# Pool tiles in PSUM for the first 32 steps, w2 sum jobs stretched and moved, batch 2 two steps later

## The chip, the cores and the metric

The kernel runs on one core of one Trainium2 chip. The metric is the device time of one execution in microseconds, as the median of several runs. Trace times count from the start of the profiled execution's span. The engines are PE (matmul), PEld (its weight loads), DVE, ACT, POOL and SP; SP and POOL also issue the DMA transfers.

## The reference

An attention with learned memory slots feeds a mixture of four experts, all in float32. Batch 8, 8 heads, sequence 576, head size 64, 32 slots; N = 4608 rows, D = 512, E = 4, F = 1024.

```python
a = softmax(phi, axis=2)                          # over the sequence, 32 slots
k_m = einsum('bhsm,bhsd->bhmd', a, k)
v_m = einsum('bhsm,bhsd->bhmd', a, v)
attn = softmax(q @ k_m.T / sqrt(64), axis=-1)
x = (attn @ v_m).transpose(0, 2, 1, 3).reshape(4608, 512)
p = domain_probs / (domain_probs.sum(-1, keepdims=True) + 1e-9)
for e in range(4):
    h = maximum(x @ w1[e], 0)
    out += p[:, e:e+1] * (h @ w2[e])
```

## The kernel before, in words

**Numbers.** Each float32 operand of a large product is split into a rounded high part (ACT, a cast) and the rest (DVE or POOL, a subtraction), and a product is three matmuls: high x high, high x low, low x high.

**Steps.** Two batches make a pair; four pairs. The first product takes attention weights times a `vw` tile (the slots' values already multiplied by w1), so `x` itself is never built. Pairs 0 and 1 run in 256 steps: 128 per pair, 32 per expert, and in an expert two batches, two halves of their columns, and eight slices `j` of F. `first(s)` (L647 to L649) makes a slice of the hidden layer for 256 or 320 columns, ACT's relu (L659) its high part `h` and DVE (L661) the low part; the piece of a 320-column step that belongs to another row tile goes to `hm`. `second(s)` (L680 to L682) multiplies `h` by w2 into output banks, and its third matmul reads the low part. `first` is emitted two steps ahead of `second`. After eight steps `accumulate` (L700, L702) adds the banks, times `p`, into `acc` on DVE. Pairs 2 and 3 come after step 256, in units of seven multiplications for eight, made from the sums of w2 blocks that are prepared earlier.

**Order.** Each engine executes its instructions in order. The emission of the first `FREE` steps is ordered by a scheduler; from there on it stands as written. `plan[s]` holds what else is emitted in step `s`, between `accumulate` of the step before, `first(s + 2)` and `second(s)`; `at(s, f)` puts something there.

**Sum jobs.** `sums(s, own, e, fh)` prepares half of an expert's w2 for the later units. SP loads two 512 KB pieces into `raw` (L208), DVE makes four sums and differences in place (L231 to L234), ACT casts four times (L220), POOL subtracts four times (L221) and stores four pieces of 512 KB (L226). An `own` job uses buffers of the attention's tiles `a`, `tl` and `ph`; the other kind takes one of the three `AT` buffers and two of the three `kvs` buffers. `JOBS` gives the step of each job's load; job n serves expert n // 2, half n % 2.

**Around them.** In stages that prepare `vw` for other pairs (one begins at step 70, one at step 230), SP loads w1 (L142), ACT and POOL split it (L156, L157), PE multiplies (L585), ACT and DVE write `vst` (L590, L591; the three `kvs` buffers) and POOL stores it (L573, `vwd`). SP brings `vwd` back into `vw` tiles, eight loads of 128 KB at a time (L624), and w2 tiles that an earlier step stored (L193).

**PSUM.** `banks` is one tile over all eight banks; `bank(tag)` hands out a bank from a list, four for `pm`, four for `p2`, and `give` returns it.

Of the kernel before, what the change touches and what calls it, by code (L numbers as in the profile page):

```python
# [9 lines left out]
F32 = mybir.dt.float32  # L10
# [9 lines left out]
P = 128  # L20
# [13 lines left out]

FREE = 36
VW_LOAD_AT = ((20, 25), (28, 32))
# [16 lines left out]
ATT = {  # L53
    2: (22, 48, (92, 96, 100), (97, 101, 104)),
    3: (38, 65, (104, 107, 110), (112, 113, 114)),
# [16 lines left out]
X_BANK, Y_BANK, AB_BANK = 4, 2, 6  # L72
JOBS = (62, 87, 99, 108, 117, PAIR + 28, PAIR + 85, PAIR + 94)
KEEP_AT, W2_AGAIN = 20, 24
# [6 lines left out]
def body(ctx: ExitStack, tc: tile.TileContext, qm, qt, kv, kvt, phi, prob, w1, w1d, w2, out):  # L81
# [3 lines left out]
    dram = pool("dram", space=DRAM)  # L85
    banks = pool("psum", space=PSUM).tile([P, 8, 512], F32, name="banks")
    idle = {"pm": deque(range(4)), "p2": deque(range(4, 8))}
    lent = {}

    def bank(tag, *shape):  # L90
        n = idle[tag].popleft()
        out = banks[:, n, :]
        m = 1
        for d in shape:
            m *= d
        names = "abcd"[:len(shape)]
        out = out[:, :m].rearrange(
            f"p ({' '.join(names)}) -> p {' '.join(names)}", **dict(zip(names, shape))
        )
        lent[id(out)] = tag, n, out  # L100
        return out

    def give(ps):
        tag, n, _ = lent.pop(id(ps))
        idle[tag].append(n)

# [89 lines left out]
    def sums(s, own, e, fh):  # L196
# [33 lines left out]
        at(s, load)  # L230
        at(s + 3, lambda: v.tensor_add(kept[1][:, :, low], kept[0][:, :, low], kept[1][:, :, low]))  # L231
        at(s + 3, lambda: sub(kept[0][:, :, low], kept[0][:, :, top], kept[0][:, :, low]))
        at(s + 4, lambda: sub(kept[0][:, :, top], kept[1][:, :, low], kept[0][:, :, top]))
        at(s + 4, lambda: sub(kept[1][:, :, top], kept[1][:, :, top], kept[0][:, :, top]))  # L234
        for i in range(2):
            for j in range(2):
                at(s + 4 + 2 * i + j, lambda i=i, j=j: high(i, j))
            at(s + 6 + 2 * i, lambda i=i: store(i))

# [470 lines left out]
    def at(s, unit):  # L710
        plan[s].append(unit if isinstance(unit, tuple) else (None, unit))
# [116 lines left out]
    for n, s in enumerate(JOBS):  # L828
        sums(s, s != PAIR + 28, n // 2, n % 2)
    for s in FIRST_LOADS:  # L830
# [384 lines left out]

    steps(0, FREE)
    with tc.manual_schedule():
        steps(FREE, BEGIN - 3)
# [61 lines left out]
```

## Time and profile before

| | us |
|---|---|
| median of 3 runs | 1411.86 (1411.23 to 1415.82) |
| profiled execution | 1409.54, span 1407.4 |
| mean granted clock | 0.994 |
| PE busy | 1366.8 (97% of the span) |
| DVE, ACT, POOL busy | 837.9, 624.8, 621.4 |

PE is the engine that is nearly always busy. In a row of waits, the three numbers are the total, the count and the longest. In a row of the timeline, the first number is the start, the second the duration, and the bracket tells how long the engine stood idle before and what ended that.

### The profile page before, as it was taken

The page shows a single profiled execution, that of the slowest core. Times are in us where ns is not written, and L with a number is a line of the kernel's source. Part 1 is how long each engine was busy: PE and PEld are TensorE (multiplying, and loading weights), DVE is VectorE, ACT ScalarE, POOL GpSimd, SP SyncE. Part 2 cuts the span into 40 slices and gives each one's busy share as a digit, 9 for nine tenths or more (in the row PEclk, how much of TensorE's full clock was granted, in tenths as well). Part 3 has the DMA queues.
Part 4 walks back from the last instruction along what each step waited for, and adds up shares of the span by engine and source line. Part 5 has one row for each costly group of instructions (what it writes and reads, how often), then busy time and mean ns, then how long its engine had stood idle before and what let it go on. Part 6 is the DMA issues. An engine that isn't in the chain of part 4 may idle for free.

```text
span 1407.4 us, 25235 instructions
## 1 busy us (share of the span) xinstructions
PE 1366.8 (97%) x8894; PEld 1250.2 (89%) x8894; DVE 837.9 (60%) x1894; ACT 624.8 (44%) x1536; POOL 621.4 (44%) x660
## 2 busy tenths in 40 slices
PE   7899999999999999999979999999999999999998
PEld 6688888888878888889868999899999999999998
DVE  7775545446754365354434467777667666666665
ACT  7654555433444364463225354555543333333332
POOL 4410344755552334422245276676763334333333
PEclk9999999999999999999989999999999999999999
DMA  7832327799684264444588898999985776666662
GB/s 252 272 104 84 123 85 246 228 354 318 226 313 163 90 226 145 139 140 124 188 272 292 278 311 289 314 315 331 321 306 154 223 190 179 177 180 177 178 177 80
DMA packets 102029, 301.37 MB, mean 214 GB/s; under 512 B 24976, under 2 KB 26128, under 8 KB 101904
## 3 DMA queue, kind: packets, MB, share of 16 engines
q1 hardware_dynamic: 81168, 224.26, 51.3%
q0 software_dynamic: 20736, 75.51, 13.8%
q8 instruction: 71, 1.16, 0.4%
q14 instruction: 54, 0.44, 0.1%
HBM read 213.46 MB, written 84.93 MB: 212 GB/s over the span
## 4 chain that ended last, share of the span: by engine, by line
PE 58%; DMA 1%; DVE 1%; ACT 0%; issue 0%; POOL 0%; SPq 0%; DVEq 0%; ACTq 0%
PE banks L1008 22%; PE banks L922 5%; PE banks L923 5%; PE banks L924 5%; PE banks L682 3%; PE banks L680 3%; PE banks L681 3%; PE banks L585 2%; PE banks L647 2%; PE banks L648 2%; PE banks L649 2%; PE banks L1046 1%; PE banks L1047 1%; PE banks L1048 1%; PE banks L469 1%; PE banks L363 1%
## 5 line engine op out<-in xcount | busy, mean ns | idle before, releaser
L1026 DVE SCALAR_TENSOR_TENSOR acc<-banks,pt,acc 128x256 f32<-128x256 f32 x416 | 200.0, 481 | 108.9 <-PE banks L1008 105.2
L157 POOL TENSOR_TENSOR w<-stage,w 128x512 fp32r<-128x512 f32 x134 | 176.6, 1323 | 166.0 <-ACT w L156 153.9
L682 PE MATMUL banks<-w,h 128*128 128x512 f32 x512 | 201.9, 395 | 14.3 <-DVE h L661 14.3
L661 DVE SCALAR_TENSOR_TENSOR h<-banks,h 128x256 fp32r<-128x256 f32 x256 | 107.6, 420 | 164.3 <-ACT h L659 101.6
L680 PE MATMUL banks<-w,h 128*128 128x512 f32 x512 | 202.2, 395 | 1.7 <-DVE acc L702 1.3
L681 PE MATMUL banks<-w,h 128*128 128x512 f32 x512 | 201.7, 394 | 0.0
L659 ACT ACTIVATE h<-banks 128x256 fp32r<-128x256 f32 x256 | 97.8, 384 | 193.1 <-PE banks L649 152.2
L647 PE MATMUL banks<-AT,vw 128*128 128x256 f32 (+1 forms) x512 | 157.4, 308 | 5.7 <-ACT kvs L351 2.2
L1008 PE MATMUL banks<-w,a 128*128 128x256 f32 x1080 | 154.6, 282 | 0.3 <-DVE acc L1026 0.2
L648 PE MATMUL banks<-AT,vw 128*128 128x256 f32 (+1 forms) x512 | 151.7, 297 | 0.0
L922 PE MATMUL banks<-AT,vw 128*128 128x256 f32 (+1 forms) x512 | 151.6, 296 | 0.0
L649 PE MATMUL banks<-AT,vw 128*128 128x256 f32 (+1 forms) x512 | 151.2, 296 | 0.1
L923 PE MATMUL banks<-AT,vw 128*128 128x256 f32 (+1 forms) x512 | 151.1, 295 | 0.0
L924 PE MATMUL banks<-AT,vw 128*128 128x256 f32 (+1 forms) x512 | 150.9, 295 | 0.0
L1008 PEld LDWEIGHTS banks<-w,a 128*128 128x128 f32 x1080 | 143.6, 188 | 4.9 <-issue 0.9
L989 POOL TENSOR_TENSOR vt<-ph,vt 128x512 fp32r<-128x512 f32 x64 | 84.1, 1314 | 107.3 <-ACT vt L988 78.3
L682 PEld LDWEIGHTS banks<-w,h 128*128 128x128 f32 x512 | 96.5, 189 | 37.4 <-DVE h L661 16.0
L352 POOL TENSOR_TENSOR kvs<-stage,kvs 128x512 fp32r<-128x512 f32 x58 | 75.8, 1325 | 101.4 <-ACT kvs L351 100.9
L647 PEld LDWEIGHTS banks<-AT,vw 128*128 128x128 f32 x512 | 97.1, 190 | 18.0 <-DVE vw L562 4.0
L680 PEld LDWEIGHTS banks<-w,h 128*128 128x128 f32 x512 | 96.6, 189 | 13.7 <-DVE acc L702 1.8
L681 PEld LDWEIGHTS banks<-w,h 128*128 128x128 f32 x512 | 96.6, 189 | 11.0
L156 ACT CAST w<-stage 128x512 fp32r<-128x512 f32 x168 | 102.7, 619 | 6.3 <-DMA stage<-in_w 4.1
(149 smaller groups left out, 2985.6 us busy)
## 6 DMA issues: line engine op xcount, KB each, us to landing
w<-kw SPq DMA_DIRECT2D x93, 512.0 KB, 5.3
vwd<-vst POOLq DMA_DIRECT2D x80, 512.0 KB, 6.2
vw<-vwd SPq DMA_DIRECT2D x320, 128.0 KB, 5.7
w<-v SPq DMA_DIRECT2D x55, 512.0 KB, 5.5
stage<-in_w SPq DMA_DIRECT2D x44, 512.0 KB, 4.3
stage<-in_w1d SPq DMA_DIRECT2D x40, 512.0 KB, 4.7
stage<-in_kv SPq DMA_DIRECT2D x32, 512.0 KB, 3.9
kw<-w POOLq DMA_DIRECT2D x32, 512.0 KB, 6.7
```

Source lines behind the costliest of these rows:

```text
L157: eng.tensor_sub(dst[:, 1, :], raw, dst[:, 0, :].bitcast(F32))
L647: nc.tensor.matmul(ps, w[:, 0, f], at_t[:, g, 0, c], start=g == 0, stop=False)
L648: nc.tensor.matmul(ps, w[:, 0, f], at_t[:, g, 1, c], start=False, stop=False)
L649: nc.tensor.matmul(ps, w[:, 1, f], at_t[:, g, 0, c], start=False, stop=g == 1)
L680: nc.tensor.matmul(po[t], x[:, 0, :], w[:, 0, :], start=j == 0, stop=False)
L681: nc.tensor.matmul(po[t], x[:, 0, :], w[:, 1, :], start=False, stop=False)
L682: nc.tensor.matmul(po[t], x[:, 1, :], w[:, 0, :], start=False, stop=j == NJ - 1)
L922: nc.tensor.matmul(ps, w[:, 0, f], at_t[:, g, 0, c], start=g == 0, stop=False)
L923: nc.tensor.matmul(ps, w[:, 0, f], at_t[:, g, 1, c], start=False, stop=False)
L924: nc.tensor.matmul(ps, w[:, 1, f], at_t[:, g, 0, c], start=False, stop=g == 1)
L1008: nc.tensor.matmul(ps, a[:, l, jj], w[:, r, c], start=start and jj + i == 0, stop=jj == 1 and i == 2, skip_group_check=True,)
L1026: VE.scalar_tensor_tensor(a, src, p, a, ALU.mult, ALU.add)
```

## The change

Four things. PSUM tiles of the first steps come from a pool with four buffers for each of two tags, `FREE` falls from 36 to 32, and after step 31 the output banks are accumulated, the pool is closed, and the one tile over all banks is opened. In a sum job DVE's operations come five and six steps after the load instead of three and four, and all that follows them two steps later. The jobs' steps change from (62, 87, 99, 108, 117, 156, 213, 222) to (60, 62, 87, 99, 111, 152, 213, 225); the job of the other kind (not `own`) was that at 156, and now those at 60 and 152 are. Batch 2's attention begins at step 24 instead of 22, its values are written at 50 instead of 48.

```diff
--- before.py
+++ after.py
@@ -32,7 +32,7 @@
 KVS = 3
 AHEAD = 2
 
-FREE = 36
+FREE = 32
 VW_LOAD_AT = ((20, 25), (28, 32))
 TURN = (0, 2, 1, 3)
 
@@ -51,7 +51,7 @@
 PAIR_AT = ((18, 19, 26, 27), (28, 29, 30, 31))
 
 ATT = {
-    2: (22, 48, (92, 96, 100), (97, 101, 104)),
+    2: (24, 50, (92, 96, 100), (97, 101, 104)),
     3: (38, 65, (104, 107, 110), (112, 113, 114)),
     4: (PAIR, PAIR + 35, (PAIR + 34, PAIR + 37, PAIR + 41), (PAIR + 38, PAIR + 42, PAIR + 45)),
     5: (PAIR + 26, PAIR + 53, (PAIR + 76, PAIR + 80, PAIR + 84), (PAIR + 112, PAIR + 113, PAIR + 114)),
@@ -70,7 +70,7 @@
 UNITS = (NG - SEVEN) * E * 2 * 4
 Q = 256
 X_BANK, Y_BANK, AB_BANK = 4, 2, 6
-JOBS = (62, 87, 99, 108, 117, PAIR + 28, PAIR + 85, PAIR + 94)
+JOBS = (60, 62, 87, 99, 111, PAIR + 24, PAIR + 85, PAIR + 97)
 KEEP_AT, W2_AGAIN = 20, 24
 FOUR_AT_7 = ((0, 4, 8, 12), (16, 20, 24, 28))
 VW_LOAD_7 = ((21, 37), (26, 41))
@@ -83,11 +83,15 @@
     pool = lambda name, **k: ctx.enter_context(tc.tile_pool(name=name, bufs=1, **k))
     const, wp, work, att = pool("const"), pool("wp"), pool("work"), pool("att")
     dram = pool("dram", space=DRAM)
-    banks = pool("psum", space=PSUM).tile([P, 8, 512], F32, name="banks")
+    early_stack = ExitStack()
+    psum = early_stack.enter_context(tc.tile_pool(name="psum", bufs=1, space=PSUM))
+    banks = None
     idle = {"pm": deque(range(4)), "p2": deque(range(4, 8))}
     lent = {}
 
     def bank(tag, *shape):
+        if banks is None:
+            return psum.tile([P, *shape], F32, name="ps", tag=tag, bufs=4)
         n = idle[tag].popleft()
         out = banks[:, n, :]
         m = 1
@@ -101,8 +105,9 @@
         return out
 
     def give(ps):
-        tag, n, _ = lent.pop(id(ps))
-        idle[tag].append(n)
+        if id(ps) in lent:
+            tag, n, _ = lent.pop(id(ps))
+            idle[tag].append(n)
 
     ident = const.tile([P, P], F32, name="ident")
     make_identity(nc, ident)
@@ -228,14 +233,14 @@
                 kept_for["v", e, fh, 2 * i + j] = d[:, j]
 
         at(s, load)
-        at(s + 3, lambda: v.tensor_add(kept[1][:, :, low], kept[0][:, :, low], kept[1][:, :, low]))
-        at(s + 3, lambda: sub(kept[0][:, :, low], kept[0][:, :, top], kept[0][:, :, low]))
-        at(s + 4, lambda: sub(kept[0][:, :, top], kept[1][:, :, low], kept[0][:, :, top]))
-        at(s + 4, lambda: sub(kept[1][:, :, top], kept[1][:, :, top], kept[0][:, :, top]))
+        at(s + 5, lambda: v.tensor_add(kept[1][:, :, low], kept[0][:, :, low], kept[1][:, :, low]))
+        at(s + 5, lambda: sub(kept[0][:, :, low], kept[0][:, :, top], kept[0][:, :, low]))
+        at(s + 6, lambda: sub(kept[0][:, :, top], kept[1][:, :, low], kept[0][:, :, top]))
+        at(s + 6, lambda: sub(kept[1][:, :, top], kept[1][:, :, top], kept[0][:, :, top]))
         for i in range(2):
             for j in range(2):
-                at(s + 4 + 2 * i + j, lambda i=i, j=j: high(i, j))
-            at(s + 6 + 2 * i, lambda i=i: store(i))
+                at(s + 6 + 2 * i + j, lambda i=i, j=j: high(i, j))
+            at(s + 8 + 2 * i, lambda i=i: store(i))
 
     def units_w1(e, fh, g):
         kept = []
@@ -826,7 +831,7 @@
         for j in range(NJ):
             at(e * STEPS + KEEP_AT + j, lambda a=(e, j): keep_w2(*a))
     for n, s in enumerate(JOBS):
-        sums(s, s != PAIR + 28, n // 2, n % 2)
+        sums(s, s not in (60, PAIR + 24), n // 2, n % 2)
     for s in FIRST_LOADS:
         at(s, lambda: load_part(wp.tile([P, 2, DM], F32R, name="w2", tag="w2", bufs=NJ + 1)))
 
@@ -1214,6 +1219,9 @@
             second(s)
 
     steps(0, FREE)
+    accumulate()
+    early_stack.close()
+    banks = pool("banks", space=PSUM).tile([P, 8, 512], F32, name="banks")
     with tc.manual_schedule():
         steps(FREE, BEGIN - 3)
         open_seven()
```

In the changed file lines have moved: L157 is L162, L193 L198, L208 L213, L221 L226, L226 L231, L231 to L234 are L236 to L239, L541 L546, L573 L578, L624 L629, L661 L666, L680 to L682 L685 to L687, L700 and L702 L705 and L707.

**Around step 32, on PE and DVE.** `ps_` tiles are the pool's, `banks_` is the one tile. PE before:

```order
L681 MATMUL banks_72<-w2_1159,h_1492 128x512
L682 MATMUL banks_72<-w2_1159,h_1492 128x512
L680 MATMUL banks_72<-w2_1159,h_1492 128x512
L681 MATMUL banks_72<-w2_1159,h_1492 128x512
L682 MATMUL banks_72<-w2_1159,h_1492 128x512
L647 MATMUL banks_72<-AT_347,vw_1335 128x256 [waits DVE_49]
L648 MATMUL banks_72<-AT_347,vw_1335 128x256
```

PE now, where the pool's last tiles meet the one tile:

```order
L687 MATMUL ps_1380<-w2_614,h_1547 128x512
L685 MATMUL ps_1384<-w2_614,h_1547 128x512
L686 MATMUL ps_1384<-w2_614,h_1547 128x512
L687 MATMUL ps_1384<-w2_614,h_1547 128x512
L546 MATMUL banks_1625<-w1_1568,vt0_81 128x512 [waits DVE_49,Activation_49]
L547 MATMUL banks_1625<-w1_1568,vt0_81 128x512
L548 MATMUL banks_1625<-w1_1568,vt0_81 128x512
L311 MATMUL banks_1625<-ident_72,ph_1365 128x128 x4
```

DVE now, at the same place:

```order
L567 TENSOR_TENSOR vw_1560<-ps_1594,vw_1560 64x512 [waits PE_49,Activation_49]
L567 TENSOR_TENSOR vw_1561<-ps_1594,vw_1561 64x512
L666 SCALAR_TENSOR_TENSOR h_1609<-ps_1602,h_1609 128x256 [waits Activation_49]
L705 TENSOR_SCALAR acc_1618<-ps_1380,pt_89 128x512 [waits PE_49]
L705 TENSOR_SCALAR acc_1618<-ps_1384,pt_89 128x512 [waits PE_49]
L567 TENSOR_TENSOR vw_1631<-banks_1625,vw_1631 64x512 [waits DVE_49,PE_49,Activation_49]
```

PE's first matmul into `banks_1625` now carries waits on DVE and ACT; ahead of DVE's first read of that tile stand the two accumulations (L705) of step 31. Before, the same tile went on through.

**Steps 68 to 72, on POOL.** `v000` to `v011` are stores of sum jobs, `w1_` rows the splits for the stage that starts at step 70. Before:

```order
L226 DMA v000_2609<-sv_2550 256x1x512
L226 DMA v000_2609<-raw_2441 256x1x512
L221 TENSOR_TENSOR raw_2441<-raw_2441,sv_2612 128x512 x2
L157 TENSOR_TENSOR w1_2649<-stage_2459,w1_2649 128x512
L226 DMA v001_2652<-sv_2612 256x1x512
L226 DMA v001_2652<-raw_2441 256x1x512
L157 TENSOR_TENSOR w1_2672<-stage_2459,w1_2672 128x512
L157 TENSOR_TENSOR w1_2701<-stage_2520,w1_2701 128x512
L573 DMA vwd03000_2721<-vst_2696 128x1024
L157 TENSOR_TENSOR w1_2728<-stage_2520,w1_2728 128x512
```

Now:

```order
L226 TENSOR_TENSOR raw_2488<-raw_2488,sv_2722 128x512
L226 TENSOR_TENSOR raw_2549<-raw_2549,sv_2727 128x512
L226 TENSOR_TENSOR raw_2488<-raw_2488,sv_2722 128x512
L226 TENSOR_TENSOR raw_2549<-raw_2549,sv_2727 128x512
L162 TENSOR_TENSOR w1_2766<-stage_2567,w1_2766 128x512
L231 DMA v001_2769<-sv_2722 256x1x512
L231 DMA v001_2769<-raw_2488 256x1x512
L231 DMA v010_2772<-sv_2727 256x1x512
L231 DMA v010_2772<-raw_2549 256x1x512
L226 TENSOR_TENSOR raw_2549<-raw_2549,sv_2775 128x512
L162 TENSOR_TENSOR w1_2795<-stage_2567,w1_2795 128x512
L226 TENSOR_TENSOR raw_2549<-raw_2549,sv_2775 128x512
```

Of the second job (`raw_2549`), which was elsewhere, two subtractions now stand ahead of the first `w1_` split and two stores, a subtraction between it and the second, and the other subtraction ahead of the third.

**The last sum job, on SP and DVE.** `raw_6969` before and `raw_7133` now are its tiles. SP before:

```order
L624 DMA vw_6925<-vwd03013_2918 32x1024
L193 DMA w2_6947<-kw235_4088 128x1024
L193 DMA w2_6967<-kw236_4115 128x1024
L208 DMA raw_6969<-in_w2 128x1024 x2
L193 DMA w2_6987<-kw237_4150 128x1024
L624 DMA vw_7006<-vwd03100_2950 32x1024
L624 DMA vw_7006<-vwd03101_2980 32x1024
```

SP now:

```order
L198 DMA w2_7044<-kw235_4208 128x1024
L198 DMA w2_7067<-kw236_4233 128x1024
L198 DMA w2_7086<-kw237_4266 128x1024
L629 DMA vw_7108<-vwd03100_3078 32x1024
L629 DMA vw_7108<-vwd03101_3108 32x1024
L629 DMA vw_7108<-vwd03102_3140 32x1024
L629 DMA vw_7108<-vwd03103_3180 32x1024
L629 DMA vw_7113<-vwd03110_3214 32x1024
L629 DMA vw_7113<-vwd03111_3246 32x1024
L629 DMA vw_7113<-vwd03112_3273 32x1024
L629 DMA vw_7113<-vwd03113_3306 32x1024
L213 DMA raw_7133<-in_w2 128x1024 x2
```

The job's load, which stood ahead of a w2 load and eight `vw` loads, now stands behind them. DVE before, from an accumulation (L702) on:

```order
L702 SCALAR_TENSOR_TENSOR acc_5112<-banks_72,pt_90,acc_5112 128x512 x2
L661 SCALAR_TENSOR_TENSOR h_7022<-banks_72,h_7022 128x256
L231 TENSOR_TENSOR raw_6969<-raw_6969 128x2x256
L232 TENSOR_TENSOR raw_6969<-raw_6969 128x2x256
L661 SCALAR_TENSOR_TENSOR h_7039<-banks_72,h_7039 128x256
L233 TENSOR_TENSOR raw_6969<-raw_6969 128x2x256
L234 TENSOR_TENSOR raw_6969<-raw_6969 128x2x256
```

DVE now, from the last `h` ahead of the job on:

```order
L666 SCALAR_TENSOR_TENSOR h_7187<-banks_1625,h_7187 128x256
L666 SCALAR_TENSOR_TENSOR h_7202<-banks_1625,h_7202 128x256
L236 TENSOR_TENSOR raw_7133<-raw_7133 128x2x256
L237 TENSOR_TENSOR raw_7133<-raw_7133 128x2x256
L666 SCALAR_TENSOR_TENSOR h_7224<-banks_1625,h_7224 128x256
L666 SCALAR_TENSOR_TENSOR hm_90<-banks_1625,hm_90 128x64
L238 TENSOR_TENSOR raw_7133<-raw_7133 128x2x256
L239 TENSOR_TENSOR raw_7133<-raw_7133 128x2x256
L666 SCALAR_TENSOR_TENSOR h_7249<-banks_1625,h_7249 128x256
```

Between that accumulation and the job's first sum stood one `h` before; now six stand there. The `h` that stands behind the first two sums is now that of the first step with 320 columns.

## The prediction

> **What bounds the kernel now.** I read the page's busy line first, then PE's idle time by what ended it, then the timeline around the largest wait.
>
> ```profile
> span 1407.4 us, 25235 instructions
> PE 1366.8 (97%) x8894; PEld 1250.2 (89%) x8894; DVE 837.9 (60%) x1894; ACT 624.8 (44%) x1536; POOL 621.4 (44%) x660
> ```
>
> PE is busy for 97% of the span and the change leaves its matmuls alone, so only PE's idle time, and time at a lower clock, can be won or lost: some 40 us.
>
> ```profile
> PE banks L682 <- DVE h L661: 14.3, 4, 9.9
> PE banks L520 <- DVE at L499: 2.7, 1, 2.7
> PE banks L585 <- POOL w L157: 0.9, 1, 0.9
> DVE raw L231 <- DMA raw<-in_w: 19.5, 2, 13.9
> ```
>
> These columns are total, times, longest. The rows are PE's waits, and the last one DVE's. The largest is one wait of 9.9 us for DVE's `h`, and DVE's longest wait is 13.9 us for the raw w2 of a sum job. The timeline joins them:
>
> ```profile
> 702.70 0.43 DVE L661 SCALAR_TENSOR_TENSOR h<-banks,h 128x256 fp32r<-128x256 f32 x1 [0.34 <-ACT h L659]
> 717.07 0.69 DVE L231 TENSOR_TENSOR raw<-raw 128x512 f32<-128x512 f32 x1 [13.94 <-DMA raw<-in_w]
> 718.40 0.42 DVE L661 SCALAR_TENSOR_TENSOR h<-banks,h 128x256 fp32r<-128x256 f32 x1
> 708.34 0.40 PE L680 MATMUL banks<-w,h 128*128 128x512 f32 x1
> 718.87 0.79 PE L682 MATMUL banks<-w,h 128*128 128x512 f32 x1 [9.90 <-DVE h L661]
> 700.45 6.48 SPq L624 DMA_DIRECT2D vw<-vwd  x8
> 707.12 0.89 SPq L193 DMA_DIRECT2D w<-kw  x2
> 708.24 1.82 SPq L208 DMA_DIRECT2D raw<-in_w  x2
> 710.16 0.38 SPq L193 DMA_DIRECT2D w<-kw  x1
> 710.58 9.53 SPq L624 DMA_DIRECT2D vw<-vwd  x8
> ```
>
> The raw load of the last job is issued at 708.24, long after DVE has reached the add that reads it (703.1). DVE works in order, so the next step's `h` stands behind that add, and PE behind `h`. The windows show the rest of the price (columns: PE, PEld, DVE, ACT, POOL busy, clock, DMA share, GB/s):
>
> ```profile
> 700.00:704.00 4.00, 4.00 (x25) 3.50 (x24) 2.17 (x4) 0.77 (x2) 0.00 (x0) 1.00 1.06 314
> 712.00:716.00 4.00, 0.00 (x0) 0.00 (x0) 0.00 (x0) 0.00 (x0) 0.00 (x0) 0.69 1.03 412
> 716.00:720.00 4.00, 1.13 (x3) 0.94 (x4) 2.87 (x5) 0.51 (x1) 0.00 (x0) 0.50 1.05 248
> 720.00:724.00 4.00, 4.00 (x15) 3.38 (x14) 1.41 (x4) 2.58 (x7) 3.72 (x5) 0.53 0.65 201
> ```
>
> After the idle stretch PE runs at half clock until about 724: 15 matmuls where 25 fit in 700 to 704 (4 x 10/25 = 1.6 us), and some 0.8 before 720. This place costs 9.9 + 1.6 + 0.8 = 12.3 us in all.
>
> **F, the last job.** Its load moves from step 222 to 225, its DVE operations from 225 to 230. One step of 256 columns takes 2.08 us:
>
> ```profile
> 700.00 0.40 PE L680 MATMUL banks<-w,h 128*128 128x512 f32 x1
> 702.08 0.40 PE L680 MATMUL banks<-w,h 128*128 128x512 f32 x1
> ```
>
> Step 227 begins at 708.34. Without the stall step 232, the first whose `h` now stands behind the adds, begins at 708.34 + 5 x 2.08 = 718.7 and needs the low half of `h` two matmuls later, at 719.2. But the load is also moved behind the second group of eight `vw` loads on SP. That group may begin once the three `w` loads are out, at 708.4 (707.12 + 0.89 + 0.38). By the first group's 6.48 us it ends at 714.9, by its own 9.53 at 717.9. One more row gives a raw load's time to landing:
>
> ```profile
> DMA to landing us min/median/max: 3.8/5.7/12.0
> ```
>
> From 714.9 + 3.8 to 717.9 + 5.7 gives 719 to 723.7. The bytes are the same as before and the DMA engines are full until 720, so the load, now last in the queue, should land when they run dry; I take 721. Two adds (0.69 each) and `h` (0.42) make 722.8, a stall of 3.6 (1.6 to 6.3). Then POOL is late: four subtractions of 1.25 us and four store issues of 0.6 (the rows below) fall among the splits that PE needs in steps 232 to 237, where they stood ahead of them before. That is 7.4 us of work. A step there takes 2.73 (262.40 to 265.13 below) and holds a split and a store of POOL's, 1.25 + 0.6, so five steps absorb 4.5, and 2.9 remain (0 to 5). The new price is 3.6 + 2.9 = 6.5, the change **-5.8** (-10.7 to +1.4; the upper end adds a second slow-clock spell of 2.4).
>
> **C, two jobs at steps 60 and 62.** The first job's DVE work stays at step 65, the second's arrives two steps on. Its POOL work falls before the first splits of the stage that begins at step 70:
>
> ```profile
> 256.57 0.78 POOL L226 DMA_DIRECT2D v<-raw  x1
> 257.16 2.75 POOL L221 TENSOR_TENSOR raw<-raw,sv 128x512 fp32r<-128x512 f32 x2
> 259.64 1.49 POOL L157 TENSOR_TENSOR w<-stage,w 128x512 fp32r<-128x512 f32 x1
> 260.86 0.92 POOL L226 DMA_DIRECT2D v<-sv  x1
> 261.46 1.04 POOL L226 DMA_DIRECT2D v<-raw  x1
> 262.05 3.02 POOL L157 TENSOR_TENSOR w<-stage,w 128x512 fp32r<-128x512 f32 x2
> 261.19 0.50 PE L585 MATMUL banks<-w,vs 128*128 128x512 f32 x1 [0.86 <-POOL w L157]
> 262.40 0.40 PE L680 MATMUL banks<-w,h 128*128 128x512 f32 x1
> 263.79 0.63 PE L585 MATMUL banks<-w,vs 128*128 128x512 f32 x2
> 265.13 0.40 PE L680 MATMUL banks<-w,h 128*128 128x512 f32 x1
> ```
>
> POOL starts one piece every 1.25 us (257.16 to 259.64 for two), a store issue every 0.6 (260.86, 261.46, 262.05). There is no room: PE already waits 0.86 us for the first split. In the new order four subtractions precede it instead of two, so it is ready 2.5 us later, at about 263.4, and PE's wait at step 72 grows by 2.5. Between it and the second split stand four store issues and one subtraction: 263.4 + 2.4 + 1.25 + 1.25 = 268.3, while PE asks at 263.79 + 2.5 = 266.3: another 2.0. The third (subtraction, split) comes at 270.8, about when PE asks; from there on the stage's slack of 0.9 a step pays the rest. With 0.1 for collisions I take **+4.6**. Lower bound 2.5, if the second wait is absorbed; upper bound 8, if the remaining subtraction and two stores (1.25 + 1.2) reach PE too and one step's slack of 0.9 is not there. [...]
>
> ```profile
> 246.91 1.71 POOL L157 TENSOR_TENSOR w<-stage,w 128x512 fp32r<-128x512 f32 x1 [0.35 <-DVE h L661]
> 247.50 1.67 DVE L232 TENSOR_TENSOR raw<-raw 128x512 f32<-128x512 f32 x1
> ```
>
> An add of 0.69 us took 1.67 here beside a POOL split. [...]
>
> **D, the job at 117.** It goes; its neighbour moves from 108 to 111, where its load comes six steps before the one that was late. DVE waited there, and PE behind it, as in F but smaller:
>
> ```profile
> 408.20 0.69 DVE L231 TENSOR_TENSOR raw<-raw 128x512 f32<-128x512 f32 x1 [5.55 <-DMA raw<-in_w]
> PE banks L682 <- DVE h L661: 2.1, 1, 2.1
> ```
>
> The second row is PE's waits from 390 to 424 alone. **-2.3** with its small clock loss taken as 0.2 (-2.6 to 0, should the job at 111 wait in turn).
>
> **B, the border at step 32.** Before, the tail of step 31's accumulation runs beside the next matmuls:
>
> ```profile
> 147.58 0.40 PE L682 MATMUL banks<-w,h 128*128 128x512 f32 x1
> 148.27 0.39 PE L682 MATMUL banks<-w,h 128*128 128x512 f32 x1
> 149.35 1.39 DVE L700 TENSOR_SCALAR acc<-banks,pt 128x512 f32<-128x512 f32 x2
> ```
>
> Now the first matmul into the one tile waits for the last read of the pool's tiles, and DVE's last two are those accumulations, 1.39 us behind an `h`. From PE's last matmul (148.27 + 0.39) to the end of the pair (150.7) are 2.1 us; DVE is full here, so the transposes' reads that moved behind the border give back 0.3. I take **+1.8**, with 0.5 if DVE runs 1.3 earlier and 3.5 if both accumulations start only when PE is done.
>
> **A, the early steps.** The scheduler orders them anew: splits of w2 and one `vw` cast trade places on ACT and DVE ahead of PE's early waits. No wait is removed for certain. The 2.7 of PE's wait for L499 is the most to win here, a pair of DVE operations of 1.4 in front of an `h` the nearest loss; I take a quarter of the gain, **-0.7**, since only one of the pieces that move stands ahead of that wait.
>
> **Moves at no price.** Attention of batch 2 two steps later, and the job at 156 going to 152 into other buffers: each issues the same work beside a busy PE (25 matmuls in a 4 us window). Uncovered, each costs one late DVE operation, 0.7; both signs are possible.
>
> **The sum.** -5.8 + 4.6 - 2.3 + 1.8 - 0.7 = -2.4. The profiled execution took 1409.54 (span 1407.4 and 2.1 around it), so 1407.1; it lies 2.3 under the runs' median of 1411.86, so as a median **1409.5**.
>
> **Rivals.**
> 1. Faster: the load lands at 719, POOL's work in both places is absorbed (C 2.5, F -10.7 with no lag), B 0.5. Then -10.7 + 2.5 - 2.3 + 0.5 - 0.7 = -10.7: 1401.2; a half way result, near 1405.5, is likelier than this end. For it: POOL is idle in every window quoted from 700 to 716, and DMA drains from 720. Against: the 0.86 wait shows no slack at step 72.
> 2. Slower: POOL's queue. PE asks for splits that stand behind subtractions and stores of the jobs, at steps 72 to 75 and 232 to 237. It decides once C passes 6 and F's stall and lag pass 11: with C 8 and F at +1.4, 8 + 1.4 - 2.3 + 1.8 - 0.7 = +8.2: 1420.1.
> 3. The move of the last job does nothing: its load, behind eight `vw` loads, is as late for step 232 as it was for 227, and the 12.3 stay. F is 0: +3.4, 1415.3; with POOL's lag behind it +6.3, 1418.2. Against: DVE asks ten microseconds later and the load perhaps eight.
> 4. The clock. Idle from 708.8, the clock fell about 713.5 (0.69 as a mean over 712 to 716), so an idle stretch of 4.7 us was borne and 3.6 should be. If the phase falls badly the 2.4 us of slow clock come too: 1411.9. [...]
>
> **Chances.** Forecast 0.36, rival 1 0.33, rival 2 0.16, rival 3 0.10, rival 4 0.05. A measurement of this kernel tells a change from none at about 0.3%, 4.2 us. Faster: rival 1 and the forecast's lower tail, 0.38. Same: the rest of the forecast, half of rival 3 and rival 4, 0.42. Slower: rival 2 and the rest of rival 3, 0.20. The forecast's own range is 1406 to 1413; over the cases 1401 to 1417 leaves some 0.1 out on each side.
>
> **What would show it.** F: the last DVE raw wait near 8 us rather than 13.9, PE's longest wait for `h` of 3 to 4, the clock at 1.00 after it, then short waits for POOL's splits at steps 234 to 237. C: two PE waits for POOL of 3.4 and 2.0 near 263 to 268. D: no wait near 407. B: one PE wait of about 2 near 148. The prediction is wrong if the raw load lands after 724 or PE never waits for POOL near 265.

## The result

The changed kernel takes 1425.61 us (median of 6 runs, 1423.07 to 1428.02) against 1413.71 (6 runs, 1411.23 to 1416.47) for the kernel before: a ratio of **1.0088, interval 1.0067 to 1.0109**, 12 us slower. The forecast was 1409.5 within 1401 to 1417, so both the sign and the range were wrong.

The profiled execution of the changed kernel took 1425.89, that of before 1409.54, 4 us under its six-run median. The two traces differ by 16.4 us of span, and the ledger below, made from them, adds up to that, not to the 12 of the medians. The page's first lines and the first rows of PE's waits (total, times, longest):

```profile
span 1423.8 us, 25216 instructions
PE 1376.5 (97%) x8894; PEld 1256.0 (88%) x8894; DVE 845.9 (59%) x1894; ACT 624.6 (44%) x1536; POOL 622.8 (44%) x660
PE banks L590 <- POOL w L162: 6.3, 4, 3.0
PE banks L687 <- DVE h L666: 5.4, 3, 4.6
PE banks L546 <- DVE acc L705: 3.1, 1, 3.1
```

The 14.3 us of waits for `h` are down to 5.4, but 5.4 came up for POOL's splits and 3.1 at the new border. PE's busy time rose by 9.7 us for the same 8894 matmuls: part of that is time at a lower clock (0.989 on average, 0.994 before).

To see where the time went I took the start of each step's `second` from both traces and followed how the difference grows:

| place | forecast | measured in the traces |
|---|---|---|
| A, up to step 31 | -0.7 | +1.3 |
| B, border at step 32 | +1.8 | +4.3 |
| C, steps 70 to 74 | +4.6 | +9.5 |
| steps 75 to 101 | 0 | +0.3 |
| D, steps 122 and 123 | -2.3 | -2.8 |
| steps 159 to 169 (the job at 152) | 0 | +2.6 |
| F, steps 228 to 240 | -5.8 | -0.3 (11.8 in place of 12.1) |
| the rest | 0 | +1.5 |

**F in the changed kernel.** DVE, PE and SP in the timeline:

```profile
728.35 0.42 DVE L666 SCALAR_TENSOR_TENSOR h<-banks,h 128x256 fp32r<-128x256 f32 x1 [1.66 <-ACT h L664]
738.76 0.69 DVE L236 TENSOR_TENSOR raw<-raw 128x512 f32<-128x512 f32 x1 [9.98 <-DMA raw<-in_w]
740.57 0.80 PE L687 MATMUL banks<-w,h 128*128 128x512 f32 x1 [4.56 <-DVE h L666]
714.15 6.96 SPq L629 DMA_DIRECT2D vw<-vwd  x8
723.60 8.62 SPq L629 DMA_DIRECT2D vw<-vwd  x8
732.39 0.98 SPq L213 DMA_DIRECT2D raw<-in_w  x2
```

Step 227 starts at 723.56 here. The raw load is issued 8.8 us after that (forecast 6.6 to 9.6) and lands 15.2 after it (forecast 12.7, at most 15.4). PE waits 4.56 us, and the clock falls (the column after POOL's):

```profile
736.00:740.00 4.00, 0.01 (x1) 0.00 (x0) 1.21 (x2) 0.00 (x0) 0.00 (x0) 0.93 0.69 275
740.00:744.00 4.00, 3.43 (x9) 2.83 (x10) 3.56 (x9) 2.68 (x7) 1.87 (x2) 0.50 0.00 0
744.00:748.00 4.00, 4.00 (x18) 3.50 (x17) 2.46 (x7) 2.60 (x8) 3.98 (x5) 0.72 0.88 294
```

The wait and the slow clock make the 6.8 us of step 232; another 5.0 follow up to step 240. Of these, 1.2 are waits for POOL's splits and 1.8 waits for DVE's `vst`, which ACT holds up while it waits for a `vwd` store to leave its buffer (4.79 us ahead of its cast at 756.63).

**C in the changed kernel.** POOL, then PE and DVE:

```profile
264.27 5.25 POOL L226 TENSOR_TENSOR raw<-raw,sv 128x512 fp32r<-128x512 f32 x4
269.25 1.48 POOL L162 TENSOR_TENSOR w<-stage,w 128x512 fp32r<-128x512 f32 x1
271.62 1.20 POOL L231 DMA_DIRECT2D v<-sv  x1
274.15 0.69 POOL L231 DMA_DIRECT2D v<-raw  x1 [1.33 <-issue]
275.97 1.38 POOL L162 TENSOR_TENSOR w<-stage,w 128x512 fp32r<-128x512 f32 x1
270.79 0.50 PE L590 MATMUL banks<-w,vs 128*128 128x512 f32 x1 [3.03 <-POOL w L162]
277.41 0.50 PE L590 MATMUL banks<-w,vs 128*128 128x512 f32 x1 [2.06 <-POOL w L162]
257.33 1.27 DVE L236 TENSOR_TENSOR raw<-raw 128x512 f32<-128x512 f32 x1
258.63 1.67 DVE L237 TENSOR_TENSOR raw<-raw 128x512 f32<-128x512 f32 x1
260.56 1.43 DVE L238 TENSOR_TENSOR raw<-raw 128x512 f32<-128x512 f32 x1
262.02 1.65 DVE L239 TENSOR_TENSOR raw<-raw 128x512 f32<-128x512 f32 x1
```

The four subtractions stand in a row as the order showed, and PE waits for the two splits that were named, 3.03 and 2.06 us. What the forecast did not hold: the second job's four DVE operations take 1.27 to 1.67 us each beside POOL's work, against 0.69 alone, and `h` behind them costs steps 70 and 71 1.8 us; and the clock falls after the waits:

```profile
272.00:276.00 4.00, 3.34 (x9) 2.17 (x7) 1.19 (x3) 0.91 (x3) 2.67 (x5) 0.60 0.99 376
276.00:280.00 4.00, 2.59 (x11) 2.26 (x12) 1.21 (x3) 1.50 (x4) 4.00 (x5) 0.83 0.76 266
280.00:284.00 4.00, 4.00 (x17) 3.35 (x16) 0.95 (x3) 1.51 (x4) 4.00 (x6) 0.75 0.73 273
```

Of the 9.5, 1.8 come in steps 70 and 71, 4.2 are the waits (3.03 + 2.06 less the 0.86 of before), and the remaining 3.5 fall in steps that ran at these clocks. That fits the clock: it is at half speed from 271.8 to 275.2 and from 278.6 to 282.0, two stretches of 3.41 us with 10 matmuls each, where the next one at full clock, 282.0 to 285.4, has 20. Half of the two makes 3.4.

**B in the changed kernel.**

```profile
147.85 0.39 PE L687 MATMUL ps<-w,h 128*128 128x512 f32 x1
151.31 0.47 PE L546 MATMUL banks<-w,vt 128*128 128x512 f32 x1 [3.07 <-DVE acc L705]
148.12 1.39 DVE L567 TENSOR_TENSOR vw<-ps,vw 64x512 fp32r<-64x512 f32 x2
149.44 0.41 DVE L666 SCALAR_TENSOR_TENSOR h<-ps,h 128x256 fp32r<-128x256 f32 x1
149.77 1.39 DVE L705 TENSOR_SCALAR acc<-ps,pt 128x512 f32<-128x512 f32 x2
```

PE finishes the last pool tile at 148.2; DVE is then still on a pair of `vw` operations and an `h`, and the two accumulations end at 151.2. So both start after PE is done, which was the forecast's upper case, 3.5. The 4.3 lie above that because a stretch of half clock follows:

```profile
148.90:152.31 3.41, 1.00 (x6) 0.85 (x7) 2.26 (x4) 0.00 (x0) 0.00 (x0) 1.00 0.62 247
152.31:155.72 3.41, 3.41 (x15) 3.02 (x14) 1.80 (x3) 1.54 (x3) 0.00 (x0) 0.50 0.00 0
```

### The profile page after: what moved, and what is told of

It is laid out like the page before. It is cut to its first block, busy times and chain, and to the rows that moved or that the text cites. A ratio compares the mean times of both kernels' runs of the same rounds, so it can differ in the third digit from the quotient of the medians.

```text
span 1423.8 us, 25216 instructions
## 1 busy us (share of the span) xinstructions
PE 1376.5 (97%) x8894; PEld 1256.0 (88%) x8894; DVE 845.9 (59%) x1894; ACT 624.6 (44%) x1536; POOL 622.8 (44%) x660
## 4 chain that ended last, share of the span: by engine, by line
PE 72%; DVE 4%; DMA 2%; POOL 2%; ACT 1%; issue 1%; SPq 0%; ACTq 0%; POOLq 0%; DVEq 0%
PE banks L1013 22%; PE banks L685 6%; PE banks L687 6%; PE banks L686 6%; PE banks L927 5%; PE banks L928 5%; PE banks L929 5%; PE banks L652 3%; PE banks L653 3%; PE banks L654 3%; PE banks L590 2%; PE banks L474 2%; DMA vw<-vwd 1%; PE banks L368 1%; PE banks L1051 1%; PE banks L1052 1%
## 5 line engine op out<-in xcount | busy, mean ns | idle before, releaser
L162 POOL TENSOR_TENSOR w<-stage,w 128x512 fp32r<-128x512 f32 x134 | 177.0, 1330 | 184.2 <-ACT w L161 178.1
L666 DVE SCALAR_TENSOR_TENSOR h<-banks,h 128x256 fp32r<-128x256 f32 x222 | 93.4, 421 | 161.4 <-ACT h L664 102.9
L687 PE MATMUL banks<-w,h 128*128 128x512 f32 x448 | 178.6, 399 | 5.4 <-DVE h L666 5.4
L685 PE MATMUL banks<-w,h 128*128 128x512 f32 x448 | 178.8, 399 | 3.4 <-DVE acc L707 1.8
L686 PE MATMUL banks<-w,h 128*128 128x512 f32 x448 | 178.1, 398 | 0.0
L664 ACT ACTIVATE h<-banks 128x256 fp32r<-128x256 f32 x222 | 85.3, 385 | 191.7 <-PE banks L654 151.8
L927 PE MATMUL banks<-AT,vw 128*128 128x256 f32 (+1 forms) x512 | 151.9, 297 | 0.0
L928 PE MATMUL banks<-AT,vw 128*128 128x256 f32 (+1 forms) x512 | 151.4, 296 | 0.0
L929 PE MATMUL banks<-AT,vw 128*128 128x256 f32 (+1 forms) x512 | 151.2, 295 | 0.0
L652 PE MATMUL banks<-AT,vw 128*128 128x256 f32 (+1 forms) x444 | 136.5, 307 | 4.3 <-DVE h L666 1.9
L653 PE MATMUL banks<-AT,vw 128*128 128x256 f32 (+1 forms) x444 | 131.9, 297 | 0.0
L654 PE MATMUL banks<-AT,vw 128*128 128x256 f32 (+1 forms) x444 | 131.6, 296 | 0.0
L687 PEld LDWEIGHTS banks<-w,h 128*128 128x128 f32 x448 | 85.5, 191 | 26.3 <-DVE h L666 6.8
L596 DVE TENSOR_TENSOR vst<-banks,vst 128x512 fp32r<-128x512 f32 x80 | 55.0, 688 | 77.7 <-ACT vst L595 77.7
L979 ACT ACTIVATE a<-banks 128x512 fp32r<-128x512 f32 x64 | 38.3, 599 | 139.0 <-DVE ph L985 107.1
L685 PEld LDWEIGHTS banks<-w,h 128*128 128x128 f32 x448 | 85.4, 191 | 14.5 <-DVE acc L707 2.2
```

The lines of the kernel that those rows point to most:

```text
L162: eng.tensor_sub(dst[:, 1, :], raw, dst[:, 0, :].bitcast(F32))
L652: nc.tensor.matmul(ps, w[:, 0, f], at_t[:, g, 0, c], start=g == 0, stop=False)
L653: nc.tensor.matmul(ps, w[:, 0, f], at_t[:, g, 1, c], start=False, stop=False)
L654: nc.tensor.matmul(ps, w[:, 1, f], at_t[:, g, 0, c], start=False, stop=g == 1)
L685: nc.tensor.matmul(po[t], x[:, 0, :], w[:, 0, :], start=j == 0, stop=False)
L686: nc.tensor.matmul(po[t], x[:, 0, :], w[:, 1, :], start=False, stop=False)
```

## The experiments

Each ratio is to the kernel before, on the same chip. Differences between two ratios whose intervals overlap are read together with the traces. The five kernels below that hold all or part of the moved jobs (e2, f2, c1, c3, a1) lie between 1.0065 and 1.0076, so their ratios do not tell them from one another. What tells them apart is where the steps of one trace each lose time.

**The parts alone.** First the two halves of the change: the pool, the border and batch 2 in one kernel, the jobs in another.

```diff
 # e1_pool_att: kernel before, and
-FREE = 36
+FREE = 32
-    2: (22, 48, ...
+    2: (24, 50, ...
+    (pool tiles, accumulate, close the pool, open `banks`, as in the change)
```

> The kernel before with two parts of the change alone: pool tiles in the first 32 steps with the border at step 32, and batch 2 two steps later (its transposes at steps 30 and 31 would otherwise hold pool tiles across the border). The jobs stay as they were. Theory 1 (four separate prices, read from where the two traces part: early steps +1.3, border +4.3, steps 70 to 74 +9.5, steps 159 to 169 +2.6, steps 88 to 122 -2.5, last job -0.3 against its old 12.1): 4 to 6.5 us slower than before, one wait of about 3 us for DVE's acc at the border, and steps 70 to 74 lose no more than the 0.9 of before. Theory 2 (the delayed border is what pushes the later stages into collision): 9 to 12 us slower, with waits for POOL's splits at step 72. Theory 3 (the border is paid back later by slack): within 1.5 us.

Measured: 1416.03, ratio 1.0039 (1.002 to 1.0057). The steps up to 31 lose 2.4 (in five other runs with the same early order -0.3 to +2.4), the border 2.5 with a wait of 2.9 for DVE's `acc`, and steps 70 to 74 nothing. Theory 1: the border has a price of its own and does not push later stages into each other.

```diff
 # e2_jobs: kernel before, and
-JOBS = (62, 87, 99, 108, 117, PAIR + 28, PAIR + 85, PAIR + 94)
+JOBS = (60, 62, 87, 99, 111, PAIR + 24, PAIR + 85, PAIR + 97)   # 60 and 152 not own
-        at(s + 3, ...)  # DVE, and all behind it
+        at(s + 5, ...)
```

> The kernel before with the third and fourth part alone: the new steps of the eight jobs, and their DVE, ACT and POOL work two steps later after the load. Theory 1: 7 to 11 us slower than before (C +9.5, steps 159 to 169 +2.6, D and its surroundings -2.5, last job 0 to +1); two waits for POOL's splits of 3 and 2 us near 266 and 273, and one wait of 4 to 5 us for h in the last job. Theory 2: 0 to 3 us slower, because without the border's delay the second job's DVE work does not meet POOL's splits.

Measured: 1421.31, ratio 1.0076 (1.0055 to 1.0098), within theory 1's 7 to 11. Without any border the steps lose time at the same places: 9.3 in steps 70 to 74, -2.8 at 123, 4.3 at 159 to 169 (2.6 in the changed kernel, where no half clock follows, see the last section), waits of 3.0 us for POOL's split and of 4.8 for `h`.

```diff
 # e4_free32: kernel before, and
-FREE = 36
+FREE = 32
```

> The kernel before with FREE = 32 alone, the one tile over all banks from the start. Theory 1 (the border costs because the first matmul into a new tile waits for the last read of the old ones): within 1.5 us of before, no wait of over 1 us near 148 to 155. Rival (what costs is that steps 32 to 35 stand in the written order instead of the scheduler's): 3 to 4.5 us slower.

Measured: 1411.79, ratio 1.0011 (0.9997 to 1.0024): no difference that can be told. The step starts shift by about 1 us at the border; the 2.9 us wait is not there. The order as written is not what costs.

```diff
 # e3_batch2_alone: kernel before, and
-    2: (22, 48, ...
+    2: (24, 50, ...
```

> The kernel before with batch 2 two steps later and nothing else. Theory 1 (moving it costs nothing, the 4 us of the pool run are the border's): within 1.5 us of before and no new wait of over 1 us. Rival (part of the border's price is batch 2's work on DVE at steps 32 to 36): 2 to 3 us slower.

Measured: 1412.45, ratio 1.0015 (0.9998 to 1.0031). A wait of 0.95 for DVE's `vw` at 150.9 is new; otherwise the same. So the border's wait belongs to the tile that is opened there.

**F: the load's place, and what comes after the wait.**

```diff
 # f1_before_last_job_late: kernel before; the last job (loaded at 222)
-        at(s + 3, ...)
+        at(s + 8, ...)     # its DVE work, and all behind it, five steps later
```

> The kernel before with one edit: the last job's DVE, ACT and POOL work five steps later, its load still at step 222 ahead of the second eight vw loads. Theory 1 (in the changed kernel the load behind the eight vw loads eats the gain): the load lands near 717, DVE asks at 713.6 and the h that PE needs is due at 719.2, so the 9.9 us wait shrinks to under 0.5, the clock stays at 1.00, and POOL's subtractions among the splits cost 2 to 5: 7 to 10 us faster than before, ratio 0.993 to 0.995. Rival (POOL's work among the splits of steps 232 to 237 costs as much as the wait did): within 3 us of before.

Measured: 1406.74, ratio 0.9967 (0.9945 to 0.999): 5 us, less than theory 1's 7 to 10. The 9.9 us wait is gone and the steps win 11.6 there, but lose 4.4 at steps 229 to 232 and 4.5 more up to step 240. PE, then ACT:

```profile
716.23 0.47 PE L680 MATMUL banks<-w,h 128*128 128x512 f32 x1 [1.22 <-DMA w<-kw]
722.92 0.68 PE L680 MATMUL banks<-w,h 128*128 128x512 f32 x1 [1.91 <-DMA w<-kw]
750.72 0.47 PE L585 MATMUL banks<-w,vs 128*128 128x512 f32 x1 [2.17 <-DVE vst L591]
749.27 0.58 ACT L590 CAST vst<-banks 128x512 fp32r<-128x512 f32 x1 [5.04 <-DMA vwd<-vst]
690.00:730.00 40.00, 36.87 (x196) 31.75 (x195) 14.98 (x31) 12.25 (x31) 13.81 (x13) 0.96 0.99 290
```

POOL's queue, the rival, is not what takes most of it back: PE waits 3.1 us for DMA of the w2 tiles and 2.5 for `vst`, which through ACT waits for stores, against 0.8 for POOL's splits. After the wait of 1.91 the clock is at 0.50 from 723.0 to 726.4, some 1.7 us more. The last row is a window of that run: DMA is full (0.99) from 690 to 730. In the kernel before, the 10 us in which PE stood still were also time in which DMA caught up (its share is 1.03, its rate 412 GB/s, from 712 to 716).

```diff
 # f2_after_last_job_early: changed kernel; the last job
-load at PAIR + 97, DVE work at + 5
+load at PAIR + 94, DVE work at + 8
```

> The changed kernel with the last job's load back at step 222, ahead of the second eight vw loads, its other work where the change put it. Theory 1 (the load's place on SP cost the changed kernel its gain): no wait for the raw load, the wait of 4.6 us for h and the slow clock after it go, and 1 to 2 us waits for w2 tiles come in their place (DMA is full): 3 to 6 us faster than the changed kernel, ratio to before about 1.005. Rival (DMA carries the same bytes, and what one load wins another loses): within 2 us of the changed kernel.

Measured: 1421.35, ratio 1.0075 (1.0056 to 1.0093), against 1.0088 for the changed kernel: 2 us by the ratios, which their intervals do not separate; by that size alone the rival (within 2 us) holds. The trace shows what theory 1 named: no wait for the raw load, waits of 0.7 and 1.8 for w2 tiles, and steps 228 to 240 cost 5.9 in place of 11.8. Other places of this trace lost more than in the changed kernel's (1.1 up to step 31, 1.6 at steps 159 to 169).

If DMA is the bound there, the job itself has to go. The next kernel does the last job at 213, the one before it at 156, and the one before that at 138.

```diff
 # g1_before_job_to_138: kernel before, and
-JOBS = (62, 87, 99, 108, 117, PAIR + 28, PAIR + 85, PAIR + 94)
+JOBS = (62, 87, 99, 108, 117, 138, 156, 213)          # 138 and 156 not own
```

> The kernel before with one job fewer near step 222: the last half's w2 is prepared at 213, and the job before it takes the other kind of buffers at step 138, where DMA moves about half of what it moves from 690 to 770. Theory 1 (DMA is the bound from 690 to 770 and the last job's 3 MB are what is too much): the 9.9 us wait goes and no w2 or vst wait takes its place, some 1 to 2 us come up at steps 138 to 150: 9 to 12 us faster than before, ratio 0.992 to 0.994. Rival (what follows at steps 231 to 240 is not the job's bytes but the vw loads and stores of the stage itself): 4 to 6 us faster, as with the last job's work made late. Rival 2 (the stall only moves to step 138, where the attention of batch 4 wants the same buffers): no faster than 2 us.

Measured: 1407.52, ratio 0.9967 (0.9954 to 0.998). Steps 228 to 240 win 11.6 and lose nothing, as theory 1 on DMA has it. (With the job go its bytes and its work on DVE, ACT and POOL alike; that it is the bytes rests on f1, whose waits ended with landings.) But the job lost 8.1 us in its new place, the second rival in part:

```profile
476.81 0.62 ACT L220 CAST sv<-raw 128x512 fp32r<-128x512 f32 x1 [10.14 <-DMA v<-sv]
478.47 1.11 PE L383 MATMUL banks<-ident,xs 128*128 128x128 f32 x4 [5.12 <-DVE h L661]
```

ACT waited 10 us for one of three `kvs` buffers, which batch 4's splits share with the job's `sv`. PE's wait is 5.1 of the 8.1; the clock is at half speed for 6.8 us from 478.3 on, which is about the other 3. At step 127 these splits have not begun.

```diff
 # g2_before_job_to_127: as above, and
-JOBS = (62, 87, 99, 108, 117, 138, 156, 213)
+JOBS = (62, 87, 99, 108, 117, 127, 156, 213)          # 127 and 156 not own
```

> As the run with a job at step 138, but that job at step 127, before batch 4 wants the three kvs buffers (at 138 ACT stood 10.1 us for one of them). Theory 1 (from 690 to 770 the DMA is the bound; with the last job gone from there neither the 9.9 us wait nor the w2 and vst waits come): the 5 us wait at steps 146 is gone too, steps 228 to 240 give 11.6 and lose nothing: 9 to 12 us faster than before, ratio 0.992 to 0.994. Rival (the earlier stages have no room for a job either): a new wait of 3 us or more between steps 127 and 140, and no more than the 5 us of the run with step 138.

Measured: 1403.26, ratio 0.9943 (0.9922 to 0.9964), 8 us faster and a little short of the 9 to 12; step 133 loses 2.3, 1.6 of it a wait for ACT's `h`.

```diff
 # g3_before_127_117_late: as above, and the job at 117
-        at(s + 3, ...)
+        at(s + 5, ...)
```

> As the run beside it (a job at 127 in place of the one at 222), and the job at 117 does its DVE, ACT and POOL work two steps later, its load unmoved. Theory (the 2.1 us wait near 407 is for a load that needs about 5.6 us more than DVE gave it, while DMA is full): that wait goes, 2 to 2.5 us more than the run beside it. Rival (the work then meets that of the job at 127): no gain over the run beside it.

Measured: **1400.89, ratio 0.9935 (0.9913 to 0.9958)**, the fastest kernel here, 9.6 us under the kernel before and, by the two ratios, 1.5% under the changed one. Against the run beside it the intervals overlap. In the trace step 123 wins 2.8 as in the changed kernel and steps 124 and 125 give 2.8 back, so the rival has the better of this one. Where the 9.9 us wait stood, PE's waits from 690 to 770 are this one row. DMA is as full as ever (282 GB/s against 290 in f1), but step 240 comes 8.2 us earlier than in f1:

```profile
PE banks L680 <- DMA w<-kw: 0.7, 1, 0.7
690.00:730.00 40.00, 39.28 (x218) 34.29 (x218) 13.92 (x32) 13.55 (x35) 14.45 (x15) 1.00 0.98 282
```

**C and the job at 152.**

```diff
 # c1_after_first5_back: changed kernel, the first five jobs as before (lag 3)
-JOBS = (60, 62, 87, 99, 111, ...
+JOBS = (62, 87, 99, 108, 117, ...
```

> The changed kernel with its first five jobs put back to steps 62, 87, 99, 108, 117 with the old lag of three steps; the border, batch 2 and the last three jobs stay changed. Theory 1 (two jobs side by side ahead of the stage at step 70 cost 9.5, and taking the job from 117 won 2.8): 6 to 8 us faster than the changed kernel, that is 4 to 6 slower than before; PE's waits for POOL's splits fall to 1 in steps 70 to 74. Rival (the border's delay of 4 us alone moves the stage against its DMA): at most 2 us faster than the changed kernel.

Measured: 1419.82, ratio 1.0065 (1.0044 to 1.0087). 3 us of difference by the ratios, less than the 6 to 8; the step starts differ by 6.5 at step 240. Steps 70 to 74 lose nothing, PE's one wait there for POOL is the old 0.87, and near 412 the old wait is back with 2.75. Theory 1 by the trace; its size in the medians is not settled.

```diff
 # c3_second_job_on_dve: changed kernel, in `high`
-            nc.gpsimd.tensor_sub(kept[2][:, i, j], ...)
+            (nc.vector if s == 62 else nc.gpsimd).tensor_sub(kept[2][:, i, j], ...)
```

> The changed kernel, but the four subtractions of the job at step 62 run on DVE instead of POOL (0.69 us each there instead of 1.25). What makes steps 70 to 74 slow? Theory Q (POOL's queue: the splits stand behind the second job's subtractions): the first wait at step 72 falls from 3.0 to about 0.9 and the second from 2.1 to under 1, no slow clock follows, and 4 to 6 us come back. Theory P (DVE and POOL hold each other up, so DVE's adds of 0.69 take 1.3 to 1.7): steps 70 and 71 stay 1.8 us longer, the four more operations on DVE bring more, and the total changes by less than 2 us. Theory S (the four more store issues on POOL): the second wait stays at 2 while the first falls.

Measured: 1421.24, ratio 1.0067 (1.0048 to 1.0086). PE's waits for POOL's splits go altogether, as theory Q has it; but in the trace steps 70 to 74 still lose 8.2 of the 9.5, because one wait takes the place of both, and half clock follows it from 264.3 to 271.1. (The ratios differ by 3 us, between Q's 4 to 6 and P's under 2, and their intervals overlap.) DVE, PE, POOL:

```profile
260.51 5.00 DVE L226 TENSOR_TENSOR raw<-raw,sv 128x512 fp32r<-128x512 f32 x1
265.43 0.41 DVE L666 SCALAR_TENSOR_TENSOR h<-banks,h 128x256 fp32r<-128x256 f32 x1
265.90 0.79 PE L687 MATMUL banks<-w,h 128*128 128x512 f32 x1 [5.46 <-DVE h L666]
261.00 2.73 POOL L226 TENSOR_TENSOR raw<-raw,sv 128x512 fp32r<-128x512 f32 x2
263.45 1.50 POOL L162 TENSOR_TENSOR w<-stage,w 128x512 fp32r<-128x512 f32 x1
264.66 0.94 POOL L231 DMA_DIRECT2D v<-sv  x1
```

A subtraction that takes DVE 0.68 us alone (the other three, from 265.77 on) ends 5.00 us after it began, and 0.56 after the last of three POOL operations in a row (263.45 + 1.50 = 264.95). `h` stands behind it. So both Q and P hold in part: POOL's queue made the two waits, and DVE's help cost as much while POOL ran.

```diff
 # a1_after_job5_back: changed kernel, the sixth job
-PAIR + 24, DVE work at + 5
+PAIR + 28, DVE work at + 3
```

> The changed kernel with the job at step 152 put back to 156 with the old lag of three steps (still in the other kind of buffers). Theory 1 (at 152 its casts on ACT stand between the exponentials, the scaling of phi of batch 5 and the relu of steps 159 to 163): the waits of 1.3 us for ACT's h and 1.9 us for DVE's h near 529 and 534 go and 3 us come back. Rival (these waits come from the phase that the earlier delays set): they stay and the time is within 1.5 us of the changed kernel.

Measured: 1420.0, ratio 1.0065 (1.0047 to 1.0083). These waits of the changed kernel are not there, and steps 159 to 169 lose nothing:

```profile
530.46 0.50 PE L685 MATMUL banks<-w,h 128*128 128x512 f32 x1 [1.30 <-ACT h L664]
536.24 0.39 PE L652 MATMUL banks<-AT,vw 128*128 128x256 f32 x1 [1.94 <-DVE h L666]
```

Theory 1: the job's place (and its lag, which went back with it), not the phase. That it is the casts' order on ACT which makes them is argued from the rows around (ACT's scaling of phi at 533.88 waited 2.26 us for DVE), and was not tried by itself.

## Why the prediction was wrong

Between the sum, -2.4, and the traces, +16.4, lie 18.8 us: F makes 5.5 of them, C 4.9, the job at 152 2.6, B 2.5 and A 2.0. By its own steps:

- **D** was right: -2.3 forecast, -2.8 found, no wait near 407.
- **B** was right in its mechanism and mis-sized. "DVE is full here" was seen, but the accumulations were counted from a trace in which they ran beside PE; with the border they start after everything that DVE owes. That was the stated upper case, "both accumulations start only when PE is done": a wait of 3.07 here. In the step starts the border cost 2.5 to 2.7 in the three runs without half clock behind it (e1, c3, a1) and 4.3 to 4.4 in the three with it (the changed kernel, f2, c1). The sum had no term for the clock here.
- **C** was right in the place, the row of POOL's instructions and the two waits (4.2 of the forecast 4.5 are there, waits of 3.03 and 2.06). It failed in "with 0.1 for collisions": no row and no run shows the 0.1. The row that stood near it, an add of 1.67 us for 0.69 beside a POOL split, gives 3.9 us more on the second job's four DVE operations if each loses as much, and was left out of the sum. They took 1.27, 1.67, 1.43 and 1.65 us, 3.3 more than four times 0.69, and at most 1.8 of it reached PE. The other 3.5 are the slow clock.
- **The clock** (rival 4) got 0.05 and was wrong where it was dismissed: "an idle stretch of 4.7 us was borne and 3.6 should be". A stretch of 3.03 us at 268 to 271 was followed by half clock, and so were one of 4.56 and one of 2.06. The length of a wait alone does not decide: the 2.06 us in the changed kernel were followed by half clock, and 3.06 us at the border of a1 were not. One long stretch in the trace of before, with the clock read in windows of 4 us, was no measure of the shortest; the last section has what the traces show in its place.
- **F** failed in its sum, -5.8 against -0.3. The load's issue and landing lay inside the range worked out, at its late end; the stall came out as 4.56 in place of 3.6, the 2.9 of POOL's lag as 5.0, but for the most part of another kind, and the slow clock came on top. The deeper error is the step that took the 12.3 us as there to be won. f1, f2 and g1 tell it apart: with the wait gone and the job still there, 8.8 of 11.6 come back (f1), 5.6 of them as waits that go back to DMA landings; with the whole job gone, none do (g1). The rows of 1.03 to 1.06 for DMA's share were read as what delays one load, not as the bound of the stage behind it.
- **"Moves at no price"** failed for the job at 152, 2.6 us in the changed kernel. It was counted as the same work beside a busy PE; its new neighbours on ACT and DVE were not looked up in the order.
- **A** can't be told: -0.3 to +2.4 over six runs with the new early order, and -1.5 to +1.8 over the five runs that kept the old one (e2, f1, g1, g2, g3).

Rival 2, POOL's queue, was the right side (its place at steps 72 and 73 held) with 0.16; its other half, steps 232 to 237, was DMA and the clock more than POOL.

## What to carry to other kernels

A stall during which another resource is at 100% (DMA's share was 1.03 while PE stood still in the kernel before, and of the 11.6 us that f1 won there 8.8 were lost again) is not all to be won: ask what that resource still owes when the stall is gone, and move bytes out of the stage rather than one transfer within it. When a job is moved, list its new neighbours on every engine it uses; here each engine's order had room by busy share (DVE 59%, ACT and POOL 44%), and what decided were the buffers (`kvs`, a wait of 10.14 us in g1), DVE's longer operations beside POOL's (1.27 to 5.00 us for 0.69), and POOL's position ahead of the splits (waits of 3.03 and 2.06). In these runs a new wait of 2 or 3 us cost up to 1.7 us more when half clock followed it (4.3 in place of 2.6 for the job at 152), and whether it did went with where the wait fell, as the last section shows.

## What the runs showed of the hardware

**DVE beside POOL.** DVE's 128x512 operations on `raw` took 0.68 and 0.69 us in the changed kernel at 255.02 and 255.73, where POOL stood idle. Those at 257.33 to 262.02 took 1.27 to 1.67, with POOL's operations of 1.72 to 1.74 each at 258.01, 259.72 and 261.40 beside them (four at 264.27 took 5.25 together). In c3 one took 5.00, and ended 0.56 after the last of three POOL operations. Why it took so much longer in c3 than in the changed kernel is not shown.

**When the clock falls.** In all 14 traces the granted clock changes between 1 and 0.5 only at the edges of a grid of 3.41 us, which runs through the whole trace. In these traces the cases part by how long PE stood idle inside one interval of that grid. From 40 to 1375 us the traces hold 5432 intervals at full clock. In 38 of them PE was idle for 1.9 us or more, and each of these was followed by an interval at half clock. In 5366 it was idle for less than 1.63, and none of these was. Of the 28 between, 7 were. (Of the kernel before and the changed one alone it is 769 intervals: 6 of 1.9 or more, all followed by half clock; 757 under 1.63, none; of the 6 between, 2.) The windows below lie on the grid (the first number is PE's busy time, the third from the end the clock). The first two are of the changed kernel, the next two of the kernel before, the last two of e1:

```profile
275.19:278.60 3.41, 1.35 (x8) 1.15 (x8) 0.04 (x1) 0.66 (x2) 3.41 (x4) 1.00 0.84 285
278.60:282.01 3.41, 3.41 (x10) 2.68 (x9) 1.21 (x3) 0.85 (x3) 3.41 (x5) 0.50 0.61 233
406.33:409.74 3.41, 1.56 (x10) 1.08 (x8) 1.51 (x3) 0.00 (x0) 0.00 (x0) 1.00 1.03 405
409.74:413.15 3.41, 3.00 (x15) 2.30 (x16) 2.35 (x5) 2.50 (x6) 1.74 (x2) 1.00 1.07 413
150.42:153.83 3.41, 1.55 (x10) 1.40 (x11) 1.71 (x4) 0.54 (x1) 0.00 (x0) 1.00 0.53 205
153.83:157.25 3.42, 3.42 (x23) 3.00 (x22) 1.80 (x3) 1.78 (x5) 0.00 (x0) 1.00 0.00 0
```

The wait of 2.06 us in the changed kernel lies in one interval, and half clock follows. The 2.1 us of the kernel before are split by an edge, 1.85 on one side, and none follows. In e1 the border's wait of 2.89 is split too, 1.86 on one side, and none follows; in the changed kernel 2.41 of the 3.07 lie in one interval, and half clock follows. In a1 the border's 3.06 are split into 1.58 and 1.48, and none follows. The same holds for the job at 152: it costs 2.6 in the changed kernel, where the later of its two waits has 1.64 us idle in one interval and no half clock follows, and 4.3 in e2, f2, c1 and c3, where it does. In the kernel before, the 9.9 us begin with 1.15 in one interval, at full clock; the next one, 3.41 us, is idle throughout and still at full clock, and half clock begins at its end, at 713.53. So the clock stayed up for 4.6 of them. This is read from the traces after the fact; no run was made to test it.
